# Attention feeding a routed mixture: the rounding of x moved from ScalarE to GpSimd, the router's logits issued in two halves

## The chip, the cores and the metric

One core of one Trainium2 chip. The metric is the device time of one execution in microseconds (us). Before the change: 1829.21 us, the median of three runs (1824.64 to 1830.63). All rows below come from one profiled execution of 1827.49 us, whose span is 1825.7 us.

## What is computed

Two stages, the second fed by the first. All arrays are float32.

```python
# attention: B, H, S, D = 4, 8, 576, 64
scores = scale * np.matmul(q, k.transpose(0, 1, 3, 2))      # causal, softmax over the last axis
local = np.matmul(a, v)
mem_out = np.einsum('bhsd,bhde->bhse', q_p, M_prev) / mem_norm
x = g * mem_out + (1 - g) * local                            # as (2304, 512)
# mixture: N, D, E, F = 2304, 512, 8, 1024
P = np.exp(x @ w_gate - max)
for _ in range(8):                                           # rows, then columns
    P /= P.sum(1, keepdims=True) + 1e-09
    P /= P.sum(0, keepdims=True) + 1e-09
    P *= N / E
out = sum(P[:, e:e + 1] * (np.maximum(x @ w1[e], 0) @ w2[e]) for e in range(E))
```

## The kernel before, in words

**Precision.** Products that need float32 accuracy are made of three passes of a faster kind (fp32r): each operand is split into a rounded part and a rest, `xh` and `xl` for x, and the product is high by high, high by low and low by high. So every operand needs one rounding (a cast to fp32r) and one subtraction.

**Attention, lines 171 to 524.** The work goes in 16 pairs: one batch and two heads each. For a pair, `qkt` transposes q and k on TensorE (PE) into PSUM; ScalarE (ACT, L230) and VectorE (DVE, L231) split them. `scores` multiplies (L303), DVE adds the mask and takes a row minimum (L317), ACT takes the exponential and its row sum (L324). `scores_tail` does the same for the last 64 rows of both heads (L335, L341, L347). `t_a` and `t_b` transpose the weights (L361, L379 to L399), and ACT and DVE copy them out of PSUM in turns (L362, L367, L383 to L404). `r_stats` turns the row sums into factors on DVE (L415 to L417) and applies them to phi(q) on GpSimd (POOL; L420, L425). `r_trans` transposes the factors and phi (L433, L434, L455) and sends the factors through DRAM, so that they come back spread over the partitions in `rsb` (L438, L441, L447, all issued by SyncE). `pv` multiplies weights, values and memory into one PSUM buffer (L470 to L481), which ACT copies into `xc` (L487). `comb` scales `xc` by `rsb` on POOL (L494), rounds it into `xh` on ACT (L497) and subtracts on POOL to give `xl` (L498).

**The order.** `atoms` (L502) gives each of these functions a place in units of a pair, and a pair's atoms reach over three pairs: its loads come at -1.6, `t_a` at 0.5, `comb` at 1.45 and 1.46, in the middle of the next pair. PE executes in exactly that order. The instructions of the other engines are put in order by a scheduler that works from the same sequence and the dependences; each engine then works through its list in order. SyncE's list holds all the loads and the two legs of the factors' round trip.

**Work from the second stage inside the first.** As soon as four pairs (one batch) are done, 512 columns of x may be used. `logits` (L527) multiplies a chunk of x with the router's weights (L532, eight matmuls), ACT copies the 16 rows out into `ls` (L537), PE transposes them by four small matmuls (L541), and DVE adds the two parts into `P`. Chunk c is at 4c + 8.33: chunks 0 and 1 in the middle of pairs 8 and 12, chunk 2 behind the last pair. The first quarter of expert 0 (`first1`, L599, L605; `first2`, L625, L620) runs on three of the five chunks in the same way.

**PSUM.** One ring of six buffers, "s", serves scores, transposes and logits in the order of the program; a matmul into a buffer waits until the engines that read its last contents are done. Within a pair, the buffer of L245 (the third of `qkt`) is the one that the first `trans` filled, so it waits for that transpose's two copies, ACT's L362 and DVE's L367.

**After attention.** The router's list of tasks (`router_tasks`, L549) holds the last two chunks' logits, the maximum (two tasks) and eight rounds of `rows` and `colsum`. `tick` runs one task at fixed places of the early expert's last two chunks and then of the experts' loop (L895). `colsum` is a matmul (L572) that waits for DVE's `rows` (L566). The experts' loop (L620, L788) is the rest of the kernel and isn't touched.

Of the kernel before, what the change touches and what calls it, by code (L numbers as in the profile page):

```python
# [8 lines left out]
F32 = mybir.dt.float32  # L9
# [8 lines left out]
def kernel(  # L18
# [13 lines left out]
    nc = tc.nc  # L32
    B, H, S, D = q.shape
    NT, DM = out.shape
    E, _, F = w1.shape
# [5 lines left out]
    CHUNKS = [(c, min(512, NT - c)) for c in range(0, NT, 512)]  # L41
# [9 lines left out]
    wst_p = ctx.enter_context(tc.tile_pool(name="wst", bufs=2))  # L51
    ps = ctx.enter_context(tc.tile_pool(name="ps", bufs=1, space=PSUM))

    xh = static.tile([128, KD, NT], F32R, name="xh")
# [42 lines left out]
    def f32(ap):  # L97
        return ap.bitcast(F32)
# [72 lines left out]
    def attention():  # L171
        with ExitStack() as actx:
# [316 lines left out]
            def comb(p, grp):  # L489
                b, hp = divmod(p, HP)  # L490
                c0, w = (0, GA) if grp == 0 else (GA, GB)
                cols = slice(b * S + c0, b * S + c0 + w)
                xc = st[p].pop(("xc", grp))
                nc.gpsimd.tensor_tensor(  # L494
                    out=xc[:, 0:w], in0=xc[:, 0:w], in1=st[p]["r"][:, c0:c0 + w], op=ALU.mult
                )
                nc.scalar.copy(out=xh[:, hp, cols], in_=xc[:, 0:w])  # L497
                nc.gpsimd.tensor_tensor(  # L498
                    out=xl[:, hp, cols], in0=xc[:, 0:w], in1=f32(xh[:, hp, cols]), op=ALU.subtract
                )  # L500
# [5 lines left out]
                (0.50, t_a), (0.80, t_b), (0.70, r_stats), (0.90, r_trans),  # L506
                (0.95, lambda p: pv(p, 0)), (1.15, lambda p: pv(p, 1)),
                (1.45, lambda p: comb(p, 0)), (1.46, lambda p: comb(p, 1)),
            ]
            seq = [  # L510
                (p + ph, lambda f=f, p=p: f(p)) for p in range(NPAIR) for ph, f in atoms
            ]
            for j in range(4):
                seq.append((0.5 + 0.5 * j, lambda j=j: w_task(j)))
            for c, parts in enumerate(early_parts()):
                seq.append((4 * c + 8.33, lambda c=c: logits(c)))
                for j, f in enumerate(parts):
                    seq.append((4 * c + 5 + j // 2 + (0.33, 0.75)[j % 2], f))
            seq.append((-0.5, setup_gates))
# [4 lines left out]
                    f()  # L524


    def logits(c):  # L527
        c0, n = CHUNKS[c]
        lp = ps_t()
        for a, x in enumerate((xh, xl)):  # L530
            for kt in range(KD):
                nc.tensor.matmul(  # L532
                    out=lp[:, 0:n], lhsT=wgp[:, kt], rhs=x[:, kt, c0:c0 + n],
                    start=(a == 0 and kt == 0), stop=(a == 1 and kt == KD - 1),
                )
        ls = wst_p.tile([128, 512], F32, tag="wst", name="ls")[0:2 * E]
        nc.scalar.copy(out=ls[:, 0:n], in_=lp[0:2 * E, 0:n])  # L537
        lt = ps_t()
        nt = n // 128
        for j in range(nt):  # L540
            nc.tensor.transpose(  # L541
                lt[:, 16 * j:16 * j + 16], ls[:, 128 * j:128 * j + 128], ident[0:2 * E, 0:2 * E]
            )
        lv = lt[:, 0:16 * nt].rearrange("p (t e) -> p t e", e=2 * E)
        pv_ = P[:, c0 // 128:c0 // 128 + nt]
        nc.vector.tensor_copy(out=pv_, in_=lv[:, :, 0:E])
        nc.vector.tensor_tensor(out=pv_, in0=lv[:, :, E:2 * E], in1=pv_, op=ALU.add)

    def router_tasks():  # L549
        tasks = [lambda c=c: logits(c) for c in (3, 4)]  # L550

        def max_a():
            nc.vector.reduce_max(mx[:, 0:1], P.rearrange("p t e -> p (t e)"), axis=AX.X)

        def max_b():
            mt = ps.tile([128, 512], F32, tag="x", name="mt", bufs=1)
            nc.tensor.transpose(mt[:, 0:128], mx[:, 0:1].to_broadcast([128, 128]), ident)
            nc.vector.reduce_max(mx[:, 1:2], mt[:, 0:128], axis=AX.X)
            nc.vector.tensor_scalar_mul(mx[:, 1:2], mx[:, 1:2], -1.0)
            nc.scalar.activation(out=P, in_=P, func=AF.Exp, bias=mx[:, 1:2])  # L560

        def rows():
            nc.vector.reduce_sum(rs, P, axis=AX.X)
            nc.vector.tensor_scalar_add(rs, rs, 1e-9)
            nc.vector.reciprocal(out=rs, in_=rs)
            nc.vector.tensor_tensor(  # L566
                out=Pt, in0=P, in1=rs.unsqueeze(2).to_broadcast([128, NTILE, E]), op=ALU.mult
            )

        def colsum():  # L570
            cp = ps.tile([128, 512], F32, tag="x", name="cp", bufs=1)
            nc.tensor.matmul(  # L572
                out=cp[:, 0:NTILE * E], lhsT=ones, rhs=Pt.rearrange("p t e -> p (t e)"),
                start=True, stop=True,
            )
            nc.vector.reduce_sum(
                cs, cp[:, 0:NTILE * E].rearrange("p (t e) -> p e t", e=E), axis=AX.X
            )
            nc.vector.tensor_scalar_add(cs, cs, 1e-9)
            nc.vector.reciprocal(out=cs, in_=cs)  # L580
            nc.vector.scalar_tensor_tensor(
                out=P, in0=Pt, scalar=float(NT) / E,
                in1=cs.unsqueeze(1).to_broadcast([128, NTILE, E]), op0=ALU.mult, op1=ALU.mult,
            )

        tasks += [max_a, max_b]
        for _ in range(8):
            tasks += [rows, colsum]
        return tasks
# [47 lines left out]
    def early_parts():  # L637
        def ps_f():
            return ps.tile([128, 512], F32, tag="f", name="f", bufs=1)

        return [first_parts(c, ps_f) for c in range(NEARLY)]
# [8 lines left out]
    def experts():  # L650
# [10 lines left out]
        tcomb = [mp.tile([128, 4, 2 * HT], F32R, name=f"t{a}") for a in "hl"]  # L661
        acc = mp.tile([128, 2 * HT // 128, DM], F32, name="acc")
        tasks = router_tasks()
        tasks.reverse()

# [259 lines left out]

    setup()
    attention()
    front.close()
    experts()
# [30 lines left out]
```

## Time and profile before

| what | value |
|---|---|
| median of 3 runs | 1829.21 us (1824.64 to 1830.63) |
| the profiled execution, its span | 1827.49 us, 1825.7 us |
| PE matmul busy | 1748.1 us (96%) |
| DVE busy | 1329.2 us (73%) |
| POOL busy | 1139.8 us (62%) |
| ACT busy | 729.0 us (40%) |
| attention, as PE sees it | from 0 to about 308 us |
| TensorE clock granted over the span | 0.984 of full speed |

PE is the busy engine, so its idle time is what to look for, and the slices of the page place nearly all of it in the first fifth of the span. In a row of the timeline, the bracket at the end holds the idle time of the engine ahead of the instruction and who ended it. The granted clock is given in shares of full speed: 1.00 is 2.4 GHz, 0.50 is 1.2 GHz.

### The profile page before, as it was taken

The page shows a single profiled execution, that of the slowest core. Times are in us where ns is not written, and L with a number is a line of the kernel's source. Part 1 is how long each engine was busy: PE and PEld are TensorE (multiplying, and loading weights), DVE is VectorE, ACT ScalarE, POOL GpSimd, SP SyncE. Part 2 cuts the span into 40 slices and gives each one's busy share as a digit, 9 for nine tenths or more (in the row PEclk, how much of TensorE's full clock was granted, in tenths as well). Part 3 has the DMA queues.
Part 4 walks back from the last instruction along what each step waited for, and adds up shares of the span by engine and source line. Part 5 has one row for each costly group of instructions (what it writes and reads, how often), then busy time and mean ns, then how long its engine had stood idle before and what let it go on. Part 6 is the DMA issues. An engine that isn't in the chain of part 4 may idle for free.

```text
span 1825.7 us, 27237 instructions
## 1 busy us (share of the span) xinstructions
PE 1748.1 (96%) x9369; PEld 1538.5 (84%) x9369; DVE 1329.2 (73%) x2385; ACT 729.0 (40%) x1586; POOL 1139.8 (62%) x1091
## 2 busy tenths in 40 slices
PE   5888889799999999999999999999999999999999
PEld 4666666689899989988998999899889899988998
DVE  6867664787777777775877777777768777777776
ACT  4666565333333333323333333333333333333332
POOL 4634434666666666757666667775577777666661
PEclk8999999899999999999999999999999999999999
DMA  4433322312222222214222222222142222222221
GB/s 106 108 76 82 88 58 91 103 60 67 66 64 70 70 70 70 75 42 139 70 70 70 70 70 69 70 65 68 53 139 70 70 68 63 66 65 64 69 70 47
DMA packets 154891, 135.58 MB, mean 74 GB/s; under 512 B 71424, under 2 KB 121728, under 8 KB 154752
## 3 DMA queue, kind: packets, MB, share of 16 engines
q1 hardware_dynamic: 154320, 133.05, 24.2%
q8 instruction: 74, 1.21, 0.3%
q10 hardware_dynamic: 432, 0.79, 0.1%
q14 instruction: 65, 0.53, 0.1%
HBM read 124.28 MB, written 9.51 MB: 73 GB/s over the span
## 4 chain that ended last, share of the span: by engine, by line
PE 82%; POOL 5%; DVE 3%; issue 3%; ACT 3%; DMA 2%; SPq 1%; POOLq 0%; ACTq 0%; DVEq 0%
PE s L620 41%; PE s L788 35%; PE x L470 1%; ACT e L324 1%; DMA rsb<-rd 1%; PE s L303 1%; POOL tl L694 1%; POOL w2l L762 1%; POOL xc L494 1%; PE s L361 1%; ACT e L347 1%; POOL w1l L739 0%; PE x L475 0%; PE f L620 0%; POOL phi L425 0%
## 5 line engine op out<-in xcount | busy, mean ns | idle before, releaser
L739 POOL TENSOR_TENSOR w1l<-raw,w1h 128x512 fp32r<-128x512 f32 x267 | 368.5, 1394 | 392.9 <-ACT w1h L738 392.9
L773 DVE SCALAR_TENSOR_TENSOR hhl<-temps,hhh 128x384 fp32r<-128x384 f32 x348 | 322.7, 946 | 184.9 <-ACT hhh L772 184.5
L620 PE MATMUL s<-w2h,hhh 128*128 128x512 f32 x1116 | 435.3, 390 | 6.5 <-DVE acc L863 6.3
L620 PE MATMUL s<-w2h,hhl 128*128 128x512 f32 x1116 | 440.7, 395 | 0.0
L620 PE MATMUL s<-w2l,hhh 128*128 128x512 f32 x1116 | 440.2, 394 | 0.0
L821 DVE TENSOR_TENSOR temps<-s,temps 128x384 f32<-128x384 f32 x609 | 330.2, 555 | 128.3 <-PE s L788 83.4
L738 ACT CAST w1h<-raw 128x512 fp32r<-128x512 f32 x267 | 166.2, 622 | 610.0 <-PE s L788 295.9
L863 DVE SCALAR_TENSOR_TENSOR acc<-s,P,acc 128x512 f32<-128x512 f32 x504 | 361.2, 741 | 38.2 <-PE s L620 37.7
L762 POOL TENSOR_TENSOR w2l<-raw,w2h 128x512 fp32r<-128x512 f32 x186 | 270.3, 1472 | 26.5 <-ACT w2h L761 26.5
L620 PEld LDWEIGHTS s<-w2h,hhh 128*128 128x128 f32 x1116 | 210.2, 188 | 45.8 <-issue 7.1
L620 PEld LDWEIGHTS s<-w2h,hhl 128*128 128x128 f32 x1116 | 209.9, 188 | 44.5
L620 PEld LDWEIGHTS s<-w2l,hhh 128*128 128x128 f32 x1116 | 209.7, 188 | 38.5
L772 ACT ACTIVATE hhh<-temps 128x384 fp32r<-128x384 f32 x348 | 173.4, 520 | 171.3 <-DVE temps L821 160.4
L788 PE MATMUL s<-th,w1l 128*128 128x384 f32 x696 | 234.9, 337 | 0.0
L788 PE MATMUL s<-th,w1h 128*128 128x384 f32 x696 | 234.4, 337 | 0.0
L788 PE MATMUL s<-tl,w1h 128*128 128x384 f32 x696 | 233.8, 336 | 0.0
L788 PE MATMUL s<-xh,w1h 128*128 128x384 f32 x618 | 208.9, 338 | 4.5 <-DVE hhl L773 4.5
L788 PE MATMUL s<-xh,w1l 128*128 128x384 f32 x618 | 208.8, 338 | 0.0
L788 PE MATMUL s<-xl,w1h 128*128 128x384 f32 x618 | 208.3, 337 | 0.0
L788 PEld LDWEIGHTS s<-th,w1h 128*128 128x128 f32 x696 | 130.8, 188 | 6.8
L788 PEld LDWEIGHTS s<-tl,w1h 128*128 128x128 f32 x696 | 130.7, 188 | 6.8
L788 PEld LDWEIGHTS s<-th,w1l 128*128 128x128 f32 x696 | 130.5, 188 | 0.0
(204 smaller groups left out, 2340.1 us busy)
## 6 DMA issues: line engine op xcount, KB each, us to landing
raw<-in_moe_w_dram SPq DMA_DIRECT2D x372, 256.0 KB
rsb<-rd SPq DMA_DIRECT2D x32, 144.0 KB
ydr<-wst SPq DMA_DIRECT2D x18, 256.0 KB
acc<-ydr SPq DMA_DIRECT2D x18, 256.0 KB
qraw<-in_q_dram SPq DMA_DIRECT2D x32, 128.0 KB
kraw<-in_k_dram SPq DMA_DIRECT2D x32, 128.0 KB
vraw<-in_v_dram SPq DMA_DIRECT2D x32, 128.0 KB
out_dram<-acc SPq DMA_DIRECT2D x15, 256.0 KB
```

The lines of the kernel that those rows point to most:

```text
L303: nc.tensor.matmul(out=sp[h][:, at:at + w], lhsT=qq[x][half[h], 128 * i:128 * i + 128], rhs=kk[y][half[h], 0:w], start=(a == 0), stop=(a = ...
L324: nc.scalar.activation(out=et[:, h, 0:w], in_=et[:, h, 0:w], func=AF.Exp, scale=-1.0, bias=mn[:, c:c + 1], accum_out=sm_[:, c:c + 1],)
L347: nc.scalar.activation(out=e4[:, 0:576], in_=e4[:, 0:576], func=AF.Exp, scale=-1.0, bias=mn[:, 8:9], accum_out=sm_[:, 8:9],)
L620: nc.tensor.matmul(out=pt, lhsT=h_[:, f, cols], rhs=w[:, f], start=(n == 0), stop=(n == 5))
L738: nc.scalar.copy(out=wh[:, i:i + 2], in_=src)
L739: tt(out=wl[:, i:i + 2], in0=src, in1=f32(wh[:, i:i + 2]), op=ALU.subtract)
L762: nc.gpsimd.tensor_tensor(out=wl[:, j], in0=raws[j], in1=f32(wh[:, j]), op=ALU.subtract)
L772: nc.scalar.activation(out=hh[:, f, c], in_=src, func=AF.Relu)
L773: nc.vector.scalar_tensor_tensor(out=hl[:, f, c], in0=src, scalar=0.0, in1=f32(hh[:, f, c]), op0=ALU.max, op1=ALU.subtract,)
L788: nc.tensor.matmul(out=pt[:, 0:HT], lhsT=w[:, wi, k], rhs=x[:, k], start=(n == 0), stop=(n == total - 1),)
L821: nc.vector.tensor_tensor(out=o, in0=x, in1=y, op=ALU.add)
L863: nc.vector.scalar_tensor_tensor(out=acc[:, j], in0=pt, scalar=P[:, t_, e:e + 1], in1=acc[:, j], op0=ALU.mult, op1=ALU.add,)
```

## The change

Three edits. The cast of `comb` (L497) goes from ACT to POOL, behind POOL's own product. `logits` becomes `logits_a` (matmuls and the copy into `ls`) and `logits_b` (the small transposes and DVE's two instructions); inside attention the second half comes at 4c + 8.75, behind the next pair's `qkt` and ahead of `t_b`, and in the router's list the halves are separate tasks, so that the list has 22 in place of 20. `ls` gets a buffer of its own; before it shared two buffers ("wst") with the weights' staging and the early expert's results.

```diff
--- before.py
+++ after.py
@@ -494,7 +494,7 @@
                 nc.gpsimd.tensor_tensor(
                     out=xc[:, 0:w], in0=xc[:, 0:w], in1=st[p]["r"][:, c0:c0 + w], op=ALU.mult
                 )
-                nc.scalar.copy(out=xh[:, hp, cols], in_=xc[:, 0:w])
+                nc.gpsimd.tensor_copy(out=xh[:, hp, cols], in_=xc[:, 0:w])
                 nc.gpsimd.tensor_tensor(
                     out=xl[:, hp, cols], in0=xc[:, 0:w], in1=f32(xh[:, hp, cols]), op=ALU.subtract
                 )
@@ -513,7 +513,8 @@
             for j in range(4):
                 seq.append((0.5 + 0.5 * j, lambda j=j: w_task(j)))
             for c, parts in enumerate(early_parts()):
-                seq.append((4 * c + 8.33, lambda c=c: logits(c)))
+                seq.append((4 * c + 8.33, lambda c=c: logits_a(c)))
+                seq.append((4 * c + 8.75, lambda c=c: logits_b(c)))
                 for j, f in enumerate(parts):
                     seq.append((4 * c + 5 + j // 2 + (0.33, 0.75)[j % 2], f))
             seq.append((-0.5, setup_gates))
@@ -524,7 +525,9 @@
                     f()
 
 
-    def logits(c):
+    lsd = {}
+
+    def logits_a(c):
         c0, n = CHUNKS[c]
         lp = ps_t()
         for a, x in enumerate((xh, xl)):
@@ -533,8 +536,13 @@
                     out=lp[:, 0:n], lhsT=wgp[:, kt], rhs=x[:, kt, c0:c0 + n],
                     start=(a == 0 and kt == 0), stop=(a == 1 and kt == KD - 1),
                 )
-        ls = wst_p.tile([128, 512], F32, tag="wst", name="ls")[0:2 * E]
+        ls = wst_p.tile([128, 512], F32, tag="ls", name="ls", bufs=1)[0:2 * E]
+        lsd[c] = ls
         nc.scalar.copy(out=ls[:, 0:n], in_=lp[0:2 * E, 0:n])
+
+    def logits_b(c):
+        c0, n = CHUNKS[c]
+        ls = lsd.pop(c)
         lt = ps_t()
         nt = n // 128
         for j in range(nt):
@@ -547,7 +555,7 @@
         nc.vector.tensor_tensor(out=pv_, in0=lv[:, :, E:2 * E], in1=pv_, op=ALU.add)
 
     def router_tasks():
-        tasks = [lambda c=c: logits(c) for c in (3, 4)]
+        tasks = [lambda c=c, f=f: f(c) for c in (3, 4) for f in (logits_a, logits_b)]
 
         def max_a():
             nc.vector.reduce_max(mx[:, 0:1], P.rearrange("p t e -> p (t e)"), axis=AX.X)
```

Up to L527 the line numbers are the same in both kernels; behind it, L532 becomes L535, L537 becomes L541, and L541 becomes L549.

ACT's list in the pair whose L245 starts at 211.89 us: L487 copies the product of the pair before, L324 and L347 are exponentials, L362 and L367 copies of transposed weights.

```order
 L256 ACTIVATE tmp<-qraw_119 128x640
 L487 COPY xc<-x 128x320
-L497 CAST xh<-xc 128x256
-L497 CAST xh<-xc 128x320
 L324 ACTIVATE e,sum<-e,mn 128x256 x2
 L324 ACTIVATE e,sum<-e,mn 128x128 x2
```

The two casts are gone from between the copy and the exponentials; the same holds in the other pairs.

POOL's list in the same pair, the `comb` of pair 9 and the `r_stats` of pair 10, as the change has it.

```order
L494 TENSOR_TENSOR xc<-xc,rsb 128x256
L494 TENSOR_TENSOR xc<-xc,rsb 128x320
L497 CAST xh<-xc 128x256
L497 CAST xh<-xc 128x320
L498 TENSOR_TENSOR xl<-xc,xh 128x256
L498 TENSOR_TENSOR xl<-xc,xh 128x320
L420 TENSOR_TENSOR qn_136<-phi,rr 64x64 x2
L425 TENSOR_TENSOR phi<-phi,rr 128x512
```

The casts stand between the products and the subtractions, ahead of L420 and L425; nothing else moved in this list there.

PE's list around the logits of chunk 0, before and then with the change: L335 is the tail's scores, L361 and L379 transposes of weights, L242 to L246 the next pair's `qkt`.

```order
L335 MATMUL s<-kh,kl 128x288
L532 MATMUL s<-xh,wgp 128x512 x4
L532 MATMUL s<-xl,wgp 128x512 x4
L541 MATMUL s<-ident,ls 128x16 x4
L361 MATMUL s<-ident,e 128x128 x14
L242 MATMUL s<-ident,qraw_120 128x128 x4
L242 MATMUL s<-ident,kraw_122 128x128 x4
L245 MATMUL s<-ident,kraw_122 128x128
L246 MATMUL s<-ident,qraw_120 128x128
L379 MATMUL s<-ident,e 128x128 x4
```

```order
L335 MATMUL s<-kh,kl 128x288
L535 MATMUL s<-xh,wgp 128x512 x4
L535 MATMUL s<-xl,wgp 128x512 x4
L361 MATMUL s<-ident,e 128x128 x14
L242 MATMUL s<-ident,qraw_120 128x128 x4
L242 MATMUL s<-ident,kraw_122 128x128 x4
L245 MATMUL s<-ident,kraw_122 128x128
L246 MATMUL s<-ident,qraw_120 128x128
L549 MATMUL s<-ident,ls 128x16 x4
L379 MATMUL s<-ident,e 128x128 x4
```

The small transposes moved from ahead of L361 to behind L246.

## Rows read from the trace of the kernel before

**Rows 1.** Busy time by stretch: start:end, length, each engine's busy us, PEclk.

```profile
core 0: us, PE busy (x) PEld busy (x) DVE busy (x) ACT busy (x) POOL busy (x), PEclk, DMA share, GB/s
75.00:310.00 235.00, 204.26 (x1557) 159.47 (x1557) 156.02 (x528) 145.36 (x431) 94.66 (x122) 0.93 0.29 76
...
400.00:1800.00 1400.00, 1393.54 (x6934) 1255.82 (x6933) 1037.29 (x1511) 510.86 (x973) 950.85 (x869) 1.00 0.23 71
```

**Rows 2.** Waits of PE, 0 to 310 us: total us, times, longest.

```profile
PE s L245 <- ACT eB L362: 10.6, 5, 3.2
PE s L245 <- DVE e L367: 9.8, 4, 3.3
PE s L541 <- ACT ls L537: 7.3, 2, 3.7
```

**Rows 3.** Waits of all engines in the same stretch.

```profile
POOL xc L494 <- DMA rsb<-rd: 32.2, 13, 7.2
...
ACT xh L497 <- POOL xc L494: 28.3, 26, 3.9
```

**Rows 4.** ACT's timeline in one pair: start us, us, instruction, count.

```profile
205.00 0.40 ACT L487 COPY xc<-x 128x320 f32<-128x320 f32 x1
...
208.49 0.50 ACT L324 ACTIVATE e<-e,mn 128x256 f32<-128x256 f32 x1
...
210.25 0.76 ACT L347 ACTIVATE e<-e,mn 128x576 f32<-128x576 f32 x1
```

**Rows 5.** DVE's timeline in the same pair.

```profile
207.25 0.52 DVE L341 CUSTOM_DVE_ANT_0 e<-s,mask,mn 128x288 f32<-128x288 f32 x1
...
211.14 0.17 DVE L415 TENSOR_SCALAR rr<-sum 128x9 f32<-128x9 f32 x1 [2.75 <-ACT e L347]
...
211.68 0.28 DVE L367 COPY e<-s 128x128 f32<-128x128 f32 x1
```

**Rows 6.** POOL's timeline in the same pair.

```profile
206.54 1.55 POOL L494 TENSOR_TENSOR xc<-xc,rsb 128x256 f32<-128x256 f32 x2 [2.27 <-DMA rsb<-rd]
208.05 1.54 POOL L498 TENSOR_TENSOR xl<-xc,xh 128x256 fp32r<-128x256 f32 x2
212.58 0.66 POOL L420 TENSOR_TENSOR qn<-phi,rr 64x64 f32<-64x64 f32 x2 [2.98 <-DVE rr L416]
213.31 1.04 POOL L425 TENSOR_TENSOR phi<-phi,rr 128x512 f32<-128x512 f32 x1
```

**Rows 7.** PE's timeline in the same pair, and L245 of the next.

```profile
211.89 0.48 PE L245 MATMUL s<-ident,kraw 128*128 128x128 f32 x1 [3.09 <-ACT eB L362]
...
216.24 0.60 PE L455 MATMUL s<-ident,phi 128*128 128x128 f32 x4
...
229.59 0.33 PE L245 MATMUL s<-ident,kraw 128*128 128x128 f32 x1 [1.62 <-ACT eB L362]
```

**Rows 8.** All executions of one line: ns min/median/max, first and last start.

```profile
L115 POOL CAST w2h<-wst x2: 613/614/614, 52.2 to 54.1; 128x512 fp32r<-128x512 f32 x2
...
L278 DVE TENSOR_SCALAR rm<-rm x16: 173/986/1330, 14.2 to 278.8; 128x9 f32<-128x9 f32 x16
...
L415 DVE TENSOR_SCALAR rr<-sum x16: 173/173/950, 22.3 to 299.2; 128x9 f32<-128x9 f32 x16
```

**Rows 9.** Busy time by stretch: five after L245, two after L541, one after 229.59.

```profile
78.15:81.56 3.41, 3.32 (x18) 1.95 (x18) 3.38 (x10) 2.13 (x7) 1.04 (x1) 0.50 0.43 96
...
sum 17.06, PE 15.90 PEld 12.16 DVE 13.24 ACT 8.87 POOL 5.58; mean PE 3.18 PEld 2.43 DVE 2.65 ACT 1.77 POOL 1.12
...
166.90:173.72 6.82, 6.33 (x31) 6.30 (x32) 3.13 (x10) 2.84 (x7) 1.62 (x3) 0.50 0.07 16
...
sum 13.65, PE 12.36 PEld 12.29 DVE 6.07 ACT 5.80 POOL 3.25; mean PE 6.18 PEld 6.14 DVE 3.04 ACT 2.90 POOL 1.62
...
229.59:233.00 3.41, 3.41 (x24) 3.07 (x25) 3.40 (x12) 2.47 (x8) 1.62 (x3) 1.00 0.30 69
```

**Rows 10.** Waits of PE, 310 to 400 us.

```profile
PE cp L572 <- DVE Pt L566: 6.9, 4, 4.0
...
PE s L541 <- ACT ls L537: 1.8, 3, 0.7
```

## The prediction

> **What bounds the kernel now.** I read the stages first, then the waits of TensorE (PE), then one pair of heads instruction by instruction. Between 400 and 1800 us PE is busy for 1393.54 of 1400.00 us, with the full clock granted [rows 1]. Nothing in that stretch is changed, and since PE has no idle time there, nothing can be gained there. Between 75 and 310 us, the attention stage, PE is busy for 204.26 of 235.00 us, at 0.93 of the clock [rows 1]. What can be won is there: some 31 us of idle time, and what the lower clock costs.
>
> The waits of PE say where [rows 2]. L245, the last transposes of the next pair's k and q, waits 10.6 us for ACT's copy at L362 (5 times) and 9.8 us for DVE's copy at L367 (4 times): 20.4 us in nine waits, since its PSUM buffer is one that these two still have to empty. L541, the small transposes of the router's logits, waits 7.3 us in two. Neither ACT nor DVE is short of time, so the reader should ask what these two stood behind. ACT waits at L497, the rounding of x, for GpSimd's product at L494: 28.3 us in 26 waits. GpSimd itself had waited there for the DMA of the row factors (rsb), 32.2 us in 13 [rows 3]. So ACT, which works its list in order, stands in the middle of a pair waiting for a round trip through DRAM, with the next exponentials queued behind it.
>
> In the pair whose L245 starts at 211.89 it reads so. ACT is free at 205.40 (205.00 + 0.40). Behind the two casts the next exponential starts at 208.49, 3.1 us later, and the last one (L347) at 210.25 [rows 4]. DVE's sums (L415) follow it at 211.14, and DVE's copy L367, queued behind L415, at 211.68 [rows 5]. L245 has waited 3.09 us [rows 7].
>
> **The change, part by part.** The sum starts from the profiled execution, 1827.49 us (span 1825.7), 1.7 below the median of the runs shown.
>
> *ACT without the casts.* L347 now needs only the sums of the scores' tail, DVE's L341, which ends at 207.77 [rows 5], and four short exponentials that fit in front of it. It can start at about 207.85 in place of 210.25, so the chain through L415, L362 and L367 comes 2.4 us earlier. What is late next is that DVE chain, and behind it L415 itself. In the present trace GpSimd stands still when L415 comes, and its median is 173 ns; but it took up to 950 ns, and L278, a TENSOR_SCALAR of the same size, spans 173 to 1330 ns with a median of 986 [rows 8]. With the change L415 comes at about 208.7, while GpSimd is still busy: L494 ends at 208.09, two casts of 0.7 together follow, then the two subtractions of L498, 1.54, to 210.3 [rows 6, 8]. I let L415 lose 0 to 0.8 us, at the middle 0.4, so this wait of 3.09 shrinks by 2.0. The other eight, read in the same way (start of L347, end of L341, start of L494, never more than the wait itself), give, in order of time, 2.0 to 2.7, 2.4 to 2.7, 1.7 to 2.5, 1.0 to 1.8, 3.0 to 3.3 ahead of it and 0.8 to 1.5, 0.9 to 1.2 and 0.3 to 0.8 behind it. With its own 1.6 to 2.4 that makes 13.7 to 18.9, and I take the middle, **16 us**.
>
> The Trainium skill, "SBUF — State Buffer", section "Who interferes with whom", says that VectorE and GpSimd share a pair of ports under an exclusive lock, so that the later of two such instructions blocks for the whole of the other. By that rule alone L415 would lose the rest of the running GpSimd instruction each time, and the term would be near its lower end; the spread of L278 agrees with it.
>
> *GpSimd with the casts.* Its cast of 128x512 took 613 to 614 ns [rows 8], 1.2 ns a column, so 256 and 320 columns cost 0.31 and 0.38, 0.7 us a pair. Bounds: 0.6, if the columns count as one cast of 512, and 1.54, if they take as long as L498's two subtractions [rows 6]. The cover is the time in which GpSimd waits for r_stats: L425 ends at 214.35, 1.9 us before PE asks at 216.24 (L455) [rows 6, 7]. PE will ask about 3 us earlier, but L425 moves up too, because L415 does. In the first pairs the GpSimd chain is on the path already; I charge **1 us**. That includes the last pair, whose xl comes 0.7 later while the early expert waits for it.
>
> *Logits in halves.* In two pairs L541 waited for ls, which ACT copied only after L347. Now the transposes of the weights L361 stand in its place, and L541 comes after L246. That frees 7.3 us [rows 2]. In the two stretches behind these waits the granted clock was 0.50, that is 1.2 GHz, with PE busy for 12.36 us [rows 9], so 6.2 more. Three things take some back: L242 must now wait for ls (its buffer is that of the product), L245 for L367, and L455 for one more buffer of the ring of six. I put 1.65 a pair on that, 3.3. Term: 13.5 - 3.3 = **10.2 us**. The private buffer for ls costs nothing: no instruction waited for the shared one in these pairs.
>
> *Clock.* Behind five of the nine L245 waits, those of 2.68 to 3.26 us, the clock stood at 0.50 for 3.41 us each, PE busy for 15.90 of 17.06 [rows 9]. Half of that is lost: 8 us. After the wait of 1.62 (L245 at 229.59) the clock stayed at 1.00 [rows 7, 9]. The shortened waits are all below 1.9, so I take **8 us** whole; the bounds are 0 and 8.
>
> *Router.* The five logits are ten tasks now, so the eight row-and-column rounds start two tasks later and one round moves from the end of the early expert into the dense stretch. PE already waits for L566 there, 6.9 us in four waits, the longest 4.0 [rows 10]. One more such wait, at their mean, is 1.7, and DVE's extra work may cost as much again: 3 us, bounds 0 and 8. Two of the last three L541 waits go (1.8 us in three [rows 10]): 1.2. Term: **-1.8 us**.
>
> Sum: 16 - 1 + 10.2 + 8 - 1.8 = 31.4, and 1827.5 - 31.4 = **1796 us**.
>
> **The rivals.**
> *GpSimd takes over.* Its chain (rsb lands, L494, casts, L498, L420, L425) becomes what a shorter pair waits for, at L455 or L434, in most pairs. For it: 0.7 us more in a chain that had 1.9 us of slack in the pair shown, and PE asks earlier. Against it: L420 waited 2.98 us for DVE's sums there [rows 6], and these come earlier. It would leave about half of the first term and none of the clock's: 8 + 10.2 - 3 = 15, so 1812 us. The Trainium skill, "GPSIMD Engine Reference", section 3.1, speaks against the change: it measured a two-input add at 1.96 times VectorE's time. By that rule, with casts of twice 0.7, this rival would be the likely one; the trace has the cast of one input at 0.61 for 512 columns.
>
> *The clock falls all the same*, after waits of 1 to 2 us: minus 8, 1804 us. The row at 229.59 speaks against it.
>
> *Everything is covered*: no loss at L415, nothing at the router, half of the logits' loss: 18.9 + 11.8 + 8 = 38.7; 1789 us, and down to 1784 with the shorter waits that I left out.
>
> *Slower: the casts on GpSimd last so long that its chain sets a longer pair than now.* In the pair shown L494 starts at 206.54; 1.55, the casts, 1.54 and 1.77 for L420 and L425 must end by 216.24, so it decides from casts of 4.8 us a pair. At 7 us each of 13 pairs would lose 2.2: 1856 us. No row has a cast or a subtraction of these sizes above 1 us.
>
> *The change does not do what it says*: the DVE chain holds L245 as long as ACT did, and the router gives back the logits' gain: 1827. The end of L341 at 207.77 against L347 at 210.25 speaks against it.
>
> **How the numbers follow.** Forecast (1790 to 1802) 0.58; clock falls all the same 0.07; GpSimd takes over 0.19; everything covered 0.08; no effect 0.05; slower 0.03. The range of 1784 to 1813 takes in the bounds of the port, the clock and the router, and half of what lies around 1812. A measurement of this kernel can tell about 0.3%, 5.5 us, from no change (its runs lie 6 us apart). All cases but the last two are faster by more: faster 0.90, same 0.06, slower 0.04.
>
> **What would show it.** Right: no wait of ACT for GpSimd's L494; L245's waits together below 8 us; L541's two waits gone; the clock at 1.00 from 75 us to the end of attention; L415 at 0.2 to 0.9 us; GpSimd about 11 us busier; attention ending near 275 us. Wrong: waits at L455 or L434 for GpSimd above 5 us in total, DVE waiting for the port in the place of ACT, or waits at L566 that grow by more than 5 us.

## The result, and the profile after

| | before | after |
|---|---|---|
| median of 4 runs, side by side | 1827.01 us (1824.64 to 1830.63) | 1794.22 us (1793.08 to 1796.49) |
| ratio | | 0.9822 (95% interval 0.9806 to 0.9837) |
| the profiled execution, its span | 1827.49 us, 1825.7 us | 1794.38 us, 1792.5 us |
| last transposes of attention (PE's L433 of the last pair) start at | 301.29 us | 266.14 us |
| from there to the end of the span | 1524.4 us | 1526.4 us |

The change is faster by 32.8 us, and the forecast of 1796 us is 1.8 us off. The gain lies where the profile said that it could lie: attention ends 35.2 us earlier, and the rest of the kernel takes as long as before, within 2 us.

PE's timeline at that L433, before and after (start, us, instruction):

```profile
301.29 0.27 PE L433 MATMUL s<-ident,rr 128*9 128x128 f32 x1
```

```profile
266.14 0.27 PE L433 MATMUL s<-ident,rr 128*9 128x128 f32 x1
```

Busy time, the first lines of the page after, and then two stretches (the columns are those of [rows 1]):

```profile
PE 1739.4 (97%) x9369; PEld 1530.1 (85%) x9369; DVE 1331.6 (74%) x2385; ACT 716.9 (40%) x1554; POOL 1153.2 (64%) x1123
```

```profile
75.00:277.00 202.00, 193.78 (x1565) 149.42 (x1564) 156.31 (x526) 134.05 (x397) 106.25 (x149) 1.00 0.34 88
...
367.00:1767.00 1400.00, 1393.64 (x6932) 1256.45 (x6931) 1038.14 (x1510) 510.29 (x971) 951.80 (x869) 1.00 0.23 71
```

The stretch from 75 us to the last matmuls of attention is 33 us shorter than in [rows 1], PE is busy for 96% of it in place of 87%, and the full clock is granted throughout, 1.00 for 0.93. Between 36.7 and 313.1 us there is no stretch at a lower one. The experts' 1400 us read as before: 1393.64 against 1393.54. GpSimd (POOL) is 13.4 us busier than before, and ACT 12.1 us less busy.

PE's waits from 0 to 277 us, which answer to [rows 2] (total us, times, longest):

```profile
PE s L434 <- POOL qn L420: 6.5, 3, 5.7
...
PE s L455 <- POOL phi L425: 3.6, 6, 0.8
PE s L245 <- DVE e L367: 1.6, 5, 0.8
PE s L245 <- ACT eB L362: 1.6, 2, 0.8
...
PE s L549 <- ACT ls L541: 0.7, 1, 0.7
...
PE s L455 <- DVE P L555: 0.5, 2, 0.3
...
PE s L549 <- DVE e L367: 0.3, 1, 0.3
```

L245 waits 3.2 us in place of 20.4. The small transposes of the two chunks inside attention (now L549) wait 0.3 us, for L367, in place of 7.3. The 0.7 us belongs to chunk 2, behind the last pair, whose wait before the change is among those of [rows 10]. The two waits for GpSimd together are 10.1 us. Before, in the same view, they were 8.1:

```profile
PE s L434 <- POOL qn L420: 5.9, 2, 5.7
...
PE s L455 <- POOL phi L425: 2.2, 3, 0.8
```

So GpSimd's chain has grown a little; more than half of its 10.1 us is the one wait of 5.7 us in the first pair, which was there before.

The waits of the other engines in the same stretch, beside [rows 3]:

```profile
ACT e L324 <- DVE mn L317: 33.8, 27, 2.4
...
POOL xc L494 <- DMA rsb<-rd: 16.6, 8, 7.5
...
DVE rr L415 <- ACT e L347: 7.1, 11, 1.0
```

The group of GpSimd's L494 (busy us, mean ns, idle us ahead of it and who ended it):

```profile
L494 POOL TENSOR_TENSOR xc<-xc,rsb 128x256 f32<-128x256 f32 x16 | 12.0, 750 | 33.3 <-DMA rsb<-rd 16.6 <-ACT e L324 9.3 <-ACT xc L487 7.4
```

No row has ACT waiting for L494 any more. ACT now waits for the row minimum of the scores that come next, which is the wait it ought to have: the exponential starts when its data is there. DVE's wait for the last exponential, behind which its copy L367 is queued, is 7.1 us in 11 (longest 1.0). Before, it was:

```profile
DVE rr L415 <- ACT e L347: 30.7, 13, 4.7
```

GpSimd still stands idle ahead of L494 for 33.3 us in all, as it did before (32.2 [rows 3]). The view puts 16.6 of them down to the landing of the factors and the rest to ACT, though L494 reads nothing that L324 writes. No exponential is queued behind this wait any more.

The worked pair of the prediction, in the timeline after (start, us, instruction; in brackets the idle time ahead):

```profile
183.58 1.57 POOL L494 TENSOR_TENSOR xc<-xc,rsb 128x256 f32<-128x256 f32 x2 [2.53 <-ACT e L324]
...
184.11 0.52 DVE L341 CUSTOM_DVE_ANT_0 e<-s,mask,mn 128x288 f32<-128x288 f32 x1
...
184.73 0.78 ACT L347 ACTIVATE e<-e,mn 128x576 f32<-128x576 f32 x1
185.09 0.80 POOL L497 CAST xh<-xc 128x256 fp32r<-128x256 f32 x2
...
185.63 0.29 DVE L415 TENSOR_SCALAR rr<-sum 128x9 f32<-128x9 f32 x1 [0.40 <-ACT e L347]
185.85 1.56 POOL L498 TENSOR_TENSOR xl<-xc,xh 128x256 fp32r<-128x256 f32 x2
186.30 0.28 DVE L367 COPY e<-s 128x128 f32<-128x128 f32 x1
...
186.40 0.33 PE L245 MATMUL s<-ident,kraw 128*128 128x128 f32 x1 [0.81 <-ACT eB L362]
...
187.51 0.66 POOL L420 TENSOR_TENSOR qn<-phi,rr 64x64 f32<-64x64 f32 x2
188.25 1.05 POOL L425 TENSOR_TENSOR phi<-phi,rr 128x512 f32<-128x512 f32 x1
...
189.50 0.60 PE L455 MATMUL s<-ident,phi 128*128 128x128 f32 x4
```

ACT's L347 starts 0.10 us behind the end of DVE's L341 (184.11 + 0.52); in [rows 4, 5] it was 2.5 us behind. L245 waits 0.81 us for 3.09 [rows 7]. On GpSimd the casts take 0.80 us, L420 and L425 come behind L498 with no gap, and L425 ends at 189.30, 0.20 us before PE asks at 189.50. The slack that was 1.9 us in this pair [rows 6, 7] is nearly used up.

```profile
L497 POOL CAST xh<-xc x32: 389/429/471, 44.0 to 276.1; 128x256 fp32r<-128x256 f32 x16, 128x320 fp32r<-128x320 f32 x16
```

```profile
L415 DVE TENSOR_SCALAR rr<-sum x16: 165/310/769, 22.2 to 263.0; 128x9 f32<-128x9 f32 x16
```

These are all executions of the moved cast and of L415 (ns, smallest, median, largest), for [rows 8].

### The profile page after: what moved, and what is told of

It reads as the page before. It is cut to its first block, busy times and chain, and to the rows that moved or that the text cites. A ratio compares the mean times of both kernels' runs of the same rounds, so it can differ in the third digit from the quotient of the medians.

```text
span 1792.5 us, 27264 instructions
## 1 busy us (share of the span) xinstructions
PE 1739.4 (97%) x9369; PEld 1530.1 (85%) x9369; DVE 1331.6 (74%) x2385; ACT 716.9 (40%) x1554; POOL 1153.2 (64%) x1123
## 4 chain that ended last, share of the span: by engine, by line
PE 83%; POOL 4%; DVE 3%; issue 3%; DMA 2%; ACT 2%; SPq 1%; POOLq 0%; ACTq 0%
PE s L628 42%; PE s L796 37%; PE x L470 1%; ACT e L324 1%; PE s L303 1%; POOL tl L702 1%; DMA rsb<-rd 1%; PE f L628 1%; DVE e L317 1%; POOL phi L425 1%; POOL w2l L770 1%; DMA raw<-in_moe_w_dram 0%; POOL xc L494 0%; DMA zb<-in_z_prev_dram 0%; POOL xl L498 0%
```

## The experiments

The theory: ACT stood in its order at the cast, waiting for a DRAM round trip, and handed this wait on to the exponentials, the sums, the copies and PE. The first rivals are that it was ACT's load that mattered, and that the cast and the halves each bring what their term of the sum said. Each ratio is against the kernel before, run beside it on the same chip.

### The cast alone (e1_cast_alone)

From the kernel before, one line; the logits stay whole.

```diff
-                nc.scalar.copy(out=xh[:, hp, cols], in_=xc[:, 0:w])
+                nc.gpsimd.tensor_copy(out=xh[:, hp, cols], in_=xc[:, 0:w])
```

> The cast of x on GpSimd, the logits unsplit as before. Theory (ACT's in-order wait for rsb was the cause): all of the L245 and clock terms come, and the logits' wait at L541 shrinks too, from 3.6 to about 1.9 us a time, because ls is copied behind L347, which comes 1.7 us earlier; a wait below 2 us leaves the clock up. 1795 to 1801 us. Rival (the two edits are separate and add up): the logits' 10 us stay lost whole, 1803 to 1806 us.

Measured: 1796.07 us (1795.32 to 1799.91), ratio 0.9833 (0.9818 to 0.9848). By the ratios this one line carries 30.5 of the change's 32.5 us. By the terms of the sum it should have brought 16 - 1 + 8 = 23 us. In its trace L541's two waits in attention are 1.80 us each, about as the theory had it. The clock fell behind the first of them and not behind the second, so the theory's other half, that such a wait leaves the clock up, held once in two.

### The halves alone (e2_logits_alone)

From the kernel before: `logits_a`, `logits_b`, the buffer of `ls` and the list of 22 tasks as in the change; the cast stays on ACT.

> The logits in halves, the cast still on ACT. Theory: L245's nine waits and the low clock behind five of them stay (20 us and 8 us); in the two logits' pairs about 4 us each are saved, since ls still comes late and L242 must wait for it, and the router's longer list costs 2: 1818 to 1823 us. Rival (the logits were the main part of the gain): below 1812 us.

Measured: 1821.94 us (1820.23 to 1824.74), ratio 0.9980 (0.9965 to 0.9995): 3.7 us by the ratio, where the terms said 10.2 - 1.8 = 8.4. PE's waits from 0 to 310 us:

```profile
PE s L245 <- ACT eB L362: 11.0, 5, 3.4
PE s L245 <- DVE e L367: 9.1, 4, 3.2
...
PE s L242 <- ACT ls L541: 3.5, 2, 1.8
```

The waits of L245 stay, and half of what L541 had waited comes back at L242, since its buffer waits for `ls`, and the copy into `ls` still stands behind the casts on ACT. In this trace, of the fastest of its six runs, the two pairs with logits are 4.5 and 4.3 us shorter (L433 to L433: 16.36 and 16.53 us, before 20.85 and 20.80), attention as a whole 7.9 us. With 30.5 us for the cast alone and 3.7 for the halves alone, the two come near the 32.5 of both; what was wrong is how they share it.

### The cast on VectorE (e3_cast_on_vector)

From the change: `nc.vector.tensor_copy` in place of `nc.gpsimd.tensor_copy`. ACT is as free of the casts as in the change.

> As the change, but the cast on VectorE in place of GpSimd. Theory (what counts is which in-order engine stands at the wait for rsb): VectorE now waits there, ahead of L317 of the short tiles, so the sums come 2 us later and L347 with them; 1812 to 1835 us. Rival (what counts is that ACT has less to do): 1794 to 1799 us.

Measured: 1822.70 us (1820.49 to 1824.40), ratio 0.9973 (0.9963 to 0.9984): nearly all of the gain is gone. From 60 to 310 us PE waits:

```profile
PE s L361 <- ACT e L324: 15.5, 11, 3.0
PE s L245 <- DVE e L367: 5.9, 5, 1.7
PE s L245 <- ACT eB L362: 4.2, 4, 1.1
```

and VectorE has taken over ACT's wait at the cast (28.3 us [rows 3]):

```profile
DVE xh L497 <- POOL xc L494: 25.2, 13, 6.8
```

Behind it stand the row minima, so ACT gets them late, and the transposes L361 wait for the exponential. The casts themselves take 19.5 us on VectorE, and this run does not part that load from the wait; the next one parts the two on ACT. To take the cast from ACT is not enough; the engine that stands at the round trip must have nothing urgent behind it.

### The cast on ACT, but later (e4_cast_late_on_scalar)

From the change: the cast goes back to ACT, behind L347, tied there by a column of zeros that ACT makes from L347's sums and adds in the cast. The subtraction (L498 of the change) moves behind it, and the last pair keeps a plain copy. ACT does one small operation per pair more than before.

```diff
+                zc = ap1.tile([128, 1], F32, tag="zc", name="zc", bufs=2)
+                st[p]["zc"] = zc
+                nc.scalar.mul(zc, sm_[:, 8:9], 0.0)
...
-                nc.gpsimd.tensor_copy(out=xh[:, hp, cols], in_=xc[:, 0:w])
...
+                    nc.scalar.activation(
+                        out=xh[:, hp, cols], in_=xc[:, 0:w], func=AF.Identity,
+                        bias=st[p + 1]["zc"][:, 0:1],
+                    )
```

> As the change, but the cast stays on ACT and comes behind L347 of the next pair, held there by a column of zeros made from that row sum and added in the cast; one more small ACT instruction a pair. Theory (the wait, not the work): ACT has even more to do than before and no longer waits for GpSimd; L347 comes as early as in the change, L362 0.6 to 1.1 us later; 1795 to 1803 us. Rival (ACT's work is the cause): no better than with the logits alone, 1818 us and more.

Measured: 1797.23 us (1796.38 to 1798.43), ratio 0.9837 (0.9821 to 0.9854). L245, from 60 to 310 us:

```profile
PE s L245 <- ACT eB L365: 3.0, 4, 0.8
PE s L245 <- DVE e L370: 2.3, 3, 0.8
```

The gain is there with the casts on ACT, each longer than on GpSimd (502 to 607 ns for 389 to 471). So it was the place in ACT's list, not ACT's load; GpSimd is one of two good places, and the two differ by 3 us or less, within their intervals.

### No L415 (e5_no_L415)

From the change; leaves out the addition of 1e-9 to the row sums, so that the price of L415 beside a busy GpSimd is gone.

```diff
-                nc.vector.tensor_scalar_add(den, st[p]["sum"], 1e-9)
+                den = st[p]["sum"]
```

> As the change, without the addition of 1e-9 to the row sums (L415); the sums, of at least 1, are used as they are. Theory (L415 loses time to GpSimd's instructions, and L245 and GpSimd's L420 stand behind it): 1 to 3 us less than the change, 1791 to 1793.5 us. Rival (L416, with two operands in SBUF, meets GpSimd in its place): no difference, 1794 us.

Measured: 1792.00 us (1791.41 to 1793.07), ratio 0.9820 (0.9805 to 0.9834), not told apart from the change's 0.9822. The time lies in the theory's range, but the kernel before, run beside it, was 1.6 us faster than the one run beside the change. In the trace attention ends at 264.73 (L433 of the last pair), and in a second one without L415 (e10) at 266.44. Three profiles of the same attention with L415 have 266.14, 266.98 (e8) and 268.17 (e6). So what L415 is worth lies within what one kernel differs by from run to run; the ratios allow some 4 us either way. Nor is this a clean price of what DVE loses beside GpSimd: the next instruction of its chain, L416, has a median of 168 ns before, 218 and 354 in two profiles of the change, and 292 and 354 in the two without L415.

### A list of 20 tasks (e6_router_list_20)

From the change; the router's two late chunks run both halves in one task, as before.

```diff
-        tasks = [lambda c=c, f=f: f(c) for c in (3, 4) for f in (logits_a, logits_b)]
+        tasks = [lambda c=c: (logits_a(c), logits_b(c)) for c in (3, 4)]
```

> As the change, but the last two chunks' logits are whole again in the router's list, which has 20 tasks as before. Theory (the longer list moved one round of rows and columns into the dense stretch, at 2 us, against 1.2 us of L549's waits saved): the tail from the last pair's L433 to the end is as long as before, 1524.4 us in place of 1526.4; 1791.5 to 1793.5 us. Rival (the tail got longer because the last xl comes later): 1794 us or more.

Measured: 1793.66 us (1791.22 to 1795.19), ratio 0.9827 (0.9812 to 0.9842): no difference that can be told. From the last L433 to the end its profile takes 1524.7 us, as the theory had it; but the change's own two profiles take 1526.4 and 1522.4, so that shows nothing. What the longer list does to the router's waits stands in the reasons below.

### The cast twice (e7_cast_twice)

From the change; the same cast is issued a second time, with the same result.

```diff
                 nc.gpsimd.tensor_copy(out=xh[:, hp, cols], in_=xc[:, 0:w])
+                nc.gpsimd.tensor_copy(out=xh[:, hp, cols], in_=xc[:, 0:w])
```

> As the change, with each cast done twice on GpSimd, 0.8 us more a pair. Theory (with the change GpSimd's chain ends just ahead of L455 in about nine pairs, 0.05 to 0.3 us): L455 waits for it there, 4 to 7 us more than the change, 1798 to 1802 us, the clock staying up. Rival (GpSimd, busy for half of this stage, has room): 1794 to 1795.5 us.

Measured: 1799.05 us (1796.22 to 1801.14), ratio 0.9862 (0.9845 to 0.9878). PE's waits from 0 to 277 us:

```profile
PE s L434 <- POOL qn L420: 8.3, 3, 5.7
PE s L455 <- POOL phi L425: 4.7, 8, 0.8
```

Together 13.0 us, 2.9 more than in the change. By the medians the kernel is 4.8 us slower than the change, by the ratios 7.3. The profile is of the fastest of the four runs: there attention ends 4.8 us later than in the change's profile (L433 of the last pair at 270.92), and 3.9 and 2.8 later than in the other two of the same attention (e8, e6). The size was expected, the place only in part: 3.3 of the 4.8 us are there by the fourth pair (its L433 at 79.52 for 76.23), part of it a stretch of 3.41 us at 0.50 of the clock behind a wait of L434. In the later pairs of this profile 0.8 us more on GpSimd is still nearly free: twelve pairs take 1.5 us longer.

### The change, the cast alone and both small edits, side by side (e8 to e10)

The split's worth on top of the cast is a difference of a thousandth, so the change and the cast alone ran again side by side on one chip, together with the change less L415 and with 20 tasks.

> The change itself, so that the next two stand beside it on one chip. Ratio to before 0.982 to 0.983, some 1794 us.

> The kernel before with the cast alone moved to GpSimd. My theory: the halves of the logits are worth 1.5 to 3 us once the cast has moved, since what held the copy into ls was the cast in front of L347 (the last pair's L433 stood 2.5 us later than with the change); so 0.8 to 1.7 thousandths above the change's ratio. Rival, by the prediction's own term: the halves are worth 10 us by themselves, so 5 thousandths above. Third: nothing that can be told, ratios that differ by under 0.5 thousandths.

> The change without the addition at L415 (the factors lack the 1e-9) and with the router's list of 20 tasks. My theory: each is worth at most 1.5 us, so 0 to 3 us below the change on the same chip, a ratio of 0.9805 to 0.9825. Rival, by the terms of the prediction: 0.4 us in nine pairs and 1.8 at the router, 5.4 us, so a ratio near 0.979.

| kernel | median | ratio | L433 of the last pair |
|---|---|---|---|
| the change again | 1795.67 us (1791.15 to 1797.51) | 0.9825 (0.9811 to 0.9838) | 266.98 us |
| the cast alone again | 1795.55 us (1795.36 to 1799.91) | 0.9837 (0.9824 to 0.9850) | 269.58 us |
| without L415, 20 tasks | 1794.72 us (1793.78 to 1795.71) | 0.9823 (0.9810 to 0.9837) | 266.44 us |

By the ratios the halves are worth 2.2 us on top of the cast, as the theory had it and as the first pair of runs did (0.9833 less 0.9822, 2.0 us); by the traces attention ends 2.5 and 2.6 us earlier with them. The intervals overlap and the two medians here are equal, so the times exclude the rival's 10 us, but not that it is nothing; and a third profile with the halves (e6) ends attention at 268.17, only 0.4 us ahead of the earlier one without. Close to the chunks the traces part more clearly. From L433 of pair 7 to that of pair 9 and from 11 to 13 (pairs counted from 0) the profiles with the halves take 67.5, 66.3 and 67.1 us together, those without 68.9 and 69.3: 1.4 to 3.0 us. The two small edits bring nothing that can be told: the 5.4 us that the terms of the sum gave them lie outside the intervals, and no version here beats the change by a measurable amount.

The cast alone also shows why there is so little left. PE's small transposes in its two pairs, and the clock behind each:

```profile
153.17 0.42 PE L541 MATMUL s<-ident,ls 16*128 16x16 f32 x4 [1.81 <-ACT ls L537]
...
219.05 0.42 PE L541 MATMUL s<-ident,ls 16*128 16x16 f32 x4 [1.80 <-ACT ls L537]
```

```profile
153.50:156.91 3.41, 3.41 (x18) 3.39 (x17) 1.45 (x6) 1.13 (x3) 2.45 (x4) 0.50 0.00 0
...
219.47:222.88 3.41, 3.41 (x32) 3.41 (x33) 2.22 (x7) 2.34 (x7) 2.42 (x4) 1.00 0.04 9
```

With the cast gone from ACT, L541 waits 3.6 us in place of 7.3 although the logits are whole, and the clock falls once behind them, for 3.41 us, where it had stood at 0.50 for 13.65 [rows 9].

## Why the prediction was right, and where its steps were not

Term by term, attention of the profiled run, with the waits of PE from [rows 2] and from the view after. PE's busy time as a whole, from the start to the last pair's L433, before and after (columns of [rows 1]):

```profile
0.00:301.29 301.29, 248.63 (x1898) 193.17 (x1899) 209.69 (x717) 185.25 (x549) 132.82 (x174) 0.93 0.33 83
```

```profile
0.00:266.14 266.14, 238.20 (x1899) 183.45 (x1900) 210.81 (x717) 173.84 (x519) 145.01 (x205) 0.98 0.38 94
```

| term | predicted | by the rows after |
|---|---|---|
| waits of L245 | 16 | 20.4 - 3.2 = 17.2 |
| GpSimd with the casts | -1 | 8.1 - 10.1 = -2.0 |
| waits of the logits, less what comes back | 7.3 - 3.3 = 4.0 | 7.3 - 0.3 - 0.5 = 6.5 |
| other idle time of PE | none | 24.7 - 21.7 = 3.0 |
| idle time of PE in all | 19.0 | (301.29 - 248.63) - (266.14 - 238.20) = 24.7 |
| clock behind L541 and L245; after: PE's busy time | 6.2 + 8 = 14.2 | 248.63 - 238.20 = 10.4 |
| sum for attention; after: by L433 of the last pair | 33.2 | 301.29 - 266.14 = 35.15 |
| router | -1.8 | 1524.4 - 1526.4 = -2.0, not a measure of it |

**L245** was right in mechanism and size. The links of the chain were each seen: ACT's wait at L494 gone, L347 0.1 us behind L341, DVE's wait for it cut from 30.7 to 7.1 us, L245 at 0.81 in the worked pair where 3.09 - 2.0 = 1.1 was forecast. The experiment with the cast late on ACT shows that the wait in the order was the cause, and the one with the cast on VectorE agrees.

**L415** was to lose 0.4 us at the middle. Its median rose from 173 to 310 ns, so 0.14. In the worked pair it ends at 185.92, as the second cast does (185.09 + 0.80 = 185.89), which agrees with the lock that the Trainium skill, "SBUF — State Buffer", section "Who interferes with whom", describes. That L415 stood there until the cast was done is read from one pair and wasn't tried, and what it cost the kernel isn't known: leaving L415 out changed nothing that can be told, and L416 became longer as well.

**The casts** were mis-sized. The step scaled one row, 613 ns for 512 columns, down by the columns to 0.31 and 0.38, 0.7 us a pair. They take 389 to 471 ns, 0.80 in the worked pair; 13.4 us more busy time over 16 pairs is 0.84. This cost little, because GpSimd had nearly that slack. The rival in which GpSimd takes over is refuted: its waits at L434 and L455 grew by 2.0 us in all. The sign that was to speak for it, waits there above 5 us in total, was badly set: they are 10.1 us, but 8.1 of that was there before. It did stand close, with 0.20 us of slack in the worked pair, and yet the run with the cast twice, 1.6 us a pair, came to 1799.05 and not to 1812. The Trainium skill, "GPSIMD Engine Reference", section 3.1, from which the prediction took casts of twice 0.7 us, compares a two-input add on GpSimd with VectorE; the 0.7 was GpSimd's own already, so the doubling doesn't follow from it, and the trace has 0.80. In the first pairs GpSimd is waited for a little longer (L434 of the third pair 0.28 and 0.84 us in the change's two profiles, no wait before), and yet L433 of the third pair starts no later: at 61.20 and 61.80 us for 62.11.

**The clock** was right in mechanism: the full clock from 36.7 us to the end of attention (in the change's second profile there is one stretch of 3.41 us at 0.50, from 49.01). Its size was too large. The step counted half of PE's busy time in the slow stretches, 14.1 us; with the same matmuls PE's busy time fell by 10.4. The idle time fell by 24.7, where the terms for waits came to 19.0. So the sum came closer than its parts: 5.7 us too little for the waits and 3.8 too much for the clock cancel in part, and that is luck. That waits below 1.9 us would not drop it held for L245 here, but not everywhere (below).

**The logits** are the step that failed, not by its size in the sum but by its owner. The prediction took L541's two waits and the clock behind them, 13.5 us less 3.3, as what the halves would bring. But L541 waited for a copy into `ls` that ACT does behind L347, which stood behind the same casts; the prediction names L347 there, and doesn't follow it one step further. To move the cast alone takes half of these waits and most of the slow clock: it brings 30.5 us, not 23. What the halves bring on top is about 2 us, not 10.2. Both parts share one cause, and a sum that prices them one by one gives the right total only because both are in the change. Of the 3.3 us that I expected the halves to give back, the view after has 0.8: L455 waits 0.5 us for one more buffer of the ring (for DVE's L555) and L549 0.3 for L367. No wait of L242 for `ls` is in it; without the move of the cast it is there, 3.5 us.

**The router** can't be told by its time. The time from the last L433 to the end of the span, 1526.4 us in the first profile of the change, is 1789.4 - 266.98 = 1522.4 in the second: the same kernel differs by 4 us, more than the term. Its waits show two effects that nearly cancel. PE's wait for DVE (now L580 for L574) is 7.8 us in four and 8.3 in five in the change's two profiles, for 6.9 in four [rows 10]; over all runs it is 7.8 to 9.3 us in the seven profiles with the list of 22, and 6.2 to 6.9 in the five with 20. So the longer list does cost there, near the 1.7 forecast. Of the L541 waits of the last three chunks, 1.8 us, 0.7 is left: 1.1 saved where 1.2 was forecast. That DVE's extra work costs as much again, the rest of the 3 us, is not shown.

## What to carry to other kernels

When an engine waits for a DMA round trip, ask what is queued behind the waiting instruction on that engine, and give the instruction to an engine that waits for the same trip anyway, or put it behind the urgent work: each worked here, and an engine with urgent work behind it (VectorE) gave nearly all of the gain back. Before two edits are priced as separate terms, follow both of their waits back until they meet; if they meet, run each alone. And take a short operation's price from a row of its own size: scaled down from a longer one it came out too low here.

## What the runs showed of the hardware that was not expected

- GpSimd's cast does not go by its columns alone. The costliest groups of the change from 0 to 300 us, shapes apart (busy us, mean ns):

```profile
L497 POOL CAST xh<-xc 128x320 fp32r<-128x320 f32 x16 | 7.3, 458 | 0.0
L497 POOL CAST xh<-xc 128x256 fp32r<-128x256 f32 x16 | 6.4, 400 | 0.3
```

  With 613 ns for 512 columns [rows 8], a line through 256 and 512 has a slope of 0.83 ns a column and some 0.19 us that do not depend on the columns (400 - 256 x 0.83); at 320 columns it gives 453 ns, beside the 458 measured.
- A wait of one length may or may not drop TensorE's clock. In the cast alone, the wait of 1.81 us at 153.17 was followed by 3.41 us at 0.50, the one of 1.80 us at 219.05 by 1.00. In the halves alone the four waits of 2.56 to 3.43 us, all of L245, were each followed by a fall, and so was one of 1.87 us (L379 at 94.24 us), while one of 1.92 us (L245 at 112.54) was not; with the cast on VectorE a wait of 2.29 us (L361 at 128.23 us) was not. In the change's second profile the clock fell at 49.01 us, and the longest wait in the 9 us before it was 1.08 us. A forecast near 2 us needs both cases.
- The lower clock cost less than half of the time spent in it. Before, stretches of 17.06 + 13.65 = 30.71 us in all [rows 9] stood at 0.50 in attention; without them PE's busy time was 10.4 us shorter, a third of that. This is the difference of two profiles, and why it isn't half stays open.
